# Tail tokens of the first token mixing as half-row pairs, u products in another pool, the last store on ScalarE's queue

## The chip, the cores and the metric

One Trainium2 chip, one of its cores. The kernel is one launch. Its time is the device time in microseconds of one execution, as the median of several runs. A profile of one further execution comes with it.

## The reference

For 8 batches, 8 heads, 576 tokens and a head size of 64: a linear attention with cosine weights, then an MLP mixer over tokens and channels. All in float32, matmuls of the kernel in bfloat16.

```python
def _attn_ref(q, k, v):                       # q, k, v: (8, 8, 576, 64)
    theta = pi/2 * pos / S
    phi(x) = concat([relu(x) * cos(theta), relu(x) * sin(theta)], -1)   # 128 features
    kv  = einsum('bhsf,bhsd->bhfd', phi(k), v);   z = sum(phi(k), axis=2)
    num = einsum('bhsf,bhfd->bhsd', phi(q), kv)
    den = einsum('bhsf,bhf->bhs', phi(q), z)[..., None] + 1e-06
    return num / den

def _moe_ref(x, w_tok1, w_tok2, w_ch1, w_ch2):    # x: (8, 576, 512), the heads side by side
    xt = x.transpose(0, 2, 1)
    h  = relu(xt @ w_tok1) @ w_tok2               # 576 -> 256 -> 576 tokens
    u  = x + h.transpose(0, 2, 1)
    h2 = relu(u @ w_ch1) @ w_ch2                  # 512 -> 1536 -> 512 channels
    return u + h2
```

## The kernel before

**Tokens.** The 576 tokens of a batch are four chunks of 128 (ci = 0 to 3) and a tail of 64 (ci = 4, called R). A chunk's tile has tokens on the 128 partitions and 512 channels (8 heads of 64) on the free axis. The tail's 64 tokens are stored twice as broad: partitions 0 to 63 hold the tail's tokens with heads 0 to 3, partitions 64 to 127 the same tokens with heads 4 to 7, so its tile is 128 x 256. `half(g)` names the partitions of half g.

**Front and channel.** Each batch has a *front* (class `Front`: attention and token mixing) and a *channel* part (class `Channel`: channel mixing and the store). While TensorE does the channel part of batch b, the pieces of the front of batch b+1 are put between its steps. The channel part is a list of 38 steps: 12 c steps (slots C+0 to C+11; `c_main` L418: 4 matmuls of 512 columns for 128 of the 1536 hidden channels, `c_tail` L428 the same for the tail tokens, 64 columns) and then the o steps (slots O+0 and on, O = 12): chunk 0 in 6 parts of 2 matmuls (L444), the tail in two halves (L448: 12 matmuls of 256 columns, each on 64 of the array's columns), then chunks 1, 2, 3 in 6 parts each. The last batch does its tail last. `pieces()` gives each piece of the next front a slot, after which it is issued; batch 1's front (made during batch 0's channel part) has a plan of its own, `first=True`. The order on each engine is the order of issue written out here.

**The front's stages.** `feature` (L193, VectorE) makes phi(k) and phi(q); `values` casts v and stands beside a column of ones; `kv` (L213) multiplies them, for the tail with the two halves of the array's rows, two accumulators in turn; `kv_out` copies to SBUF; `q_trans` or a transposing DMA brings phi(q) to feature-major form. `num` (L252, tail L259 with 64 columns each) gives numerator and denominator of a chunk in `num_ps`; VectorE makes x from it with three operations (L265 add, L266 reciprocal, L267 multiply). `tok1` (L280, tail L284) is the first token mixing: `b1_ps[mi]`, mi = 0 and 1, each 128 of the 256 hidden tokens x 512 channels, summed over the five chunks. The tail part uses `w_tail1`, which holds the last 64 rows of w_tok1 in the partitions of half g and zeros in the others: a matmul over all 128 rows then picks half g. That is two matmuls of 256 columns per mi. `tok1_out` is the relu, on ScalarE (L290) for mi = 0 and on VectorE (L292) for mi = 1. `tok2` (L308, tail L312) is the second token mixing into `u_ps`; VectorE adds x (L315), ScalarE casts to bfloat16 (L316), and u is transposed by DMA (in the first two fronts on TensorE, `u_trans`, L322).

**Pools of PSUM.** `ps_mm` has 4 buffers: c_ps, ct_ps, o_ps, b1_ps, transposes, and u_ps for batches from 1 on. `ps_at` has 2: kv_ps, num_ps, large transposes, and u_ps in the first front. 

**The first front** (batch 0, `first_front`) has no channel part beside it. It keeps TensorE occupied with matmuls on zeros (L163) while the first loads come, and runs num of one chunk, then tok1 of the chunk before it.

**Slots of the token mixing before**, batches 2 to 7: num of chunks 0, 1, 2 after C+9, C+10, C+11, of the tail after O+1, of chunk 3 after O+3; tok1 of all but chunk 3 after O+4 (mi = 0) and O+5 (mi = 1); tok1 of chunk 3 and the relus after O+6; tok2 from O+8 to O+12.

**Stores.** Each output chunk is added on VectorE (L454) and stored by a DMA issued by SP (L456); the tail's two halves are two DMAs, both issued by SP (L460).

Of the kernel before, what the change touches and what calls it, by code (L numbers as in the profile page):

```python
# [10 lines left out]
BF16 = mybir.dt.bfloat16  # L11
# [5 lines left out]
def kernel(  # L17
# [15 lines left out]
    nc = tc.nc  # L33

    B, H, S, D = q.shape
    F = 2 * D
    Dm = H * D
    S_tok, D_tok = moe_w_tok1.shape
    Dm2, D_ch = moe_w_ch1.shape
    P = 128  # L40
    R = S // P
    SM = R * P
    ST = S - SM
    NSC = R + 1
    NCC = Dm // P
    NT = D_tok // P
# [3 lines left out]
    DH = Dm // 2  # L50
    assert S_tok == S and Dm2 == Dm and F == P and 2 * ST == P and H == 2 * HH


    ORDER = (0, 1, 2, R, 3)

    def half(g):
        return slice(g * ST, (g + 1) * ST)


    const = ctx.enter_context(tc.tile_pool(name="const", bufs=1))  # L60
# [3 lines left out]
    once = ctx.enter_context(tc.tile_pool(name="once", bufs=1))  # L64
# [59 lines left out]

    w_tok1 = const.tile([P, R, D_tok], BF16, name="w_tok1")

    w_tail1 = const.tile([P, 2, D_tok], BF16, name="w_tail1")
    for g in range(2):
        nc.vector.memset(w_tail1[half(1 - g), g, :], 0.0)
    w_tok2n = const.tile([P, NT, S], BF16, name="w_tok2n")  # L130
    w_tok2 = const.tile([P, NT, S], BF16, name="w_tok2")
    w_ch1 = const.tile([P, NCC, D_ch], BF16, name="w_ch1")
    w_ch2 = const.tile([P, NCH, Dm], BF16, name="w_ch2")
    for g in range(2):
        nc.gpsimd.dma_start(out=w_tail1[half(g), g, :], in_=moe_w_tok1[SM:S, :])
    after(nc.gpsimd.dma_start(out=w_tok1,
                              in_=moe_w_tok1[0:SM, :].rearrange("(p r) t -> p r t", r=R)),
          k_done)
# [32 lines left out]
    class Front:  # L171
# [96 lines left out]
                self.x[:, ci, 0:n * DH].rearrange("p (g j d) -> p g j d", g=n, j=HH),  # L268
                nv[:, :, :, 0:D], den.to_broadcast([P, n, HH, D]))

        def tok1(self, mi, chunks):
            if not hasattr(self, "B1"):
                self.B1 = once.tile([P, NT, Dm], BF16, name="B1")
                self.b1_ps = {}
            if mi not in self.b1_ps:
                self.b1_ps[mi] = ps_mm.tile([P, Dm], F32, name="b1_ps", tag="mm")
            cols = slice(mi * P, (mi + 1) * P)
            for ci in chunks:
                if ci < R:
                    nc.tensor.matmul(self.b1_ps[mi], w_tok1[:, ci, cols], self.x[:, ci, :],  # L280
                                     start=(ci == 0), stop=(ci == R - 1))
                else:
                    for g in range(2):
                        nc.tensor.matmul(self.b1_ps[mi][:, g * DH:(g + 1) * DH],  # L284
                                         w_tail1[:, g, cols], self.x[:, R, 0:DH],
                                         start=False, stop=False, skip_group_check=True)

        def tok1_out(self, mi, on_act=True):
            if on_act:
# [60 lines left out]
            self.values(ci, nc.vector)  # L350
            self.q_side(ci)

        def mix_head(self, mi):
            self.tok1(mi, ORDER[:-1])

        def mix_tail(self):
            for mi in range(NT):
                self.tok1(mi, ORDER[-1:])
                self.tok1_out(mi, on_act=(mi == 0))

        def pieces(self, first=False):


            F, V, KV, N = self.features, self.values, self.kv, self.num
            KS, QS, QT, T, U = self.k_side, self.q_side, self.q_trans, self.tok2, self.u_trans
            C, O = 0, NCH
            if first:

                plan = [(C + 2, KS, 0), (C + 2, KS, 1), (C + 3, KS, 2), (C + 3, KS, 3),
                        (C + 4, KS, 4), (C + 4, V, 0, nc.vector), (C + 4, V, 1, nc.vector)]  # L370
                plan += [(C + 5, V, ci, nc.vector) for ci in (2, 3, 4)]
                plan += [(C + 6 + ci, KV, ci) for ci in range(NSC)]
                plan += [(C + 7 + ci, QS, ci, ci % 2 == 1) for ci in range(NSC)]
                plan.append((C + 10, self.kv_out))
                plan += [(C + at, QT, ci) for ci, at in enumerate((9, 10, 11, 12, 13))]
            else:
                plan = [(C + ci, V, ci, nc.scalar) for ci in range(NSC)]
                plan += [(C + at, KS, ci) for ci, at in enumerate((0, 0, 1, 2, 2))]
                for ci, at in enumerate((1, 2, 3, 4, 5)):
                    plan += [(C + at, QS, ci), (C + at, self.q_trans_dma, ci)]  # L380
                plan += [(C + at, KV, ci) for ci, at in enumerate((2, 3, 4, 6, 7))]
                plan.append((C + 8, self.kv_out))
            if first:
                plan += [(O + at, N, ci) for ci, at in zip(ORDER, (2, 4, 7, 9, 11))]
                mix, t = O + 13, O + 17
            else:
                plan += [(at, N, ci) for ci, at in zip(ORDER, (C + 9, C + 10, C + 11, O + 1, O + 3))]
                mix, t = O + 4, O + 8
            plan += [(mix, self.mix_head, 0), (mix + 1, self.mix_head, 1),
                     (mix + 2, self.mix_tail)]  # L390
            if first:
                plan += [(t, T, 0), (t + 1, T, 1), (t + 2, T, 2), (t + 3, U, 0), (t + 3, T, 3),
                         (t + 4, U, 1), (t + 4, T, 4), (t + 5, U, 2), (t + 6, U, 3),
                         (t + 7, U, 4)]
            else:
                plan += [(t + ci, T, ci) for ci in range(NSC)]
                plan += [(t + 1, self.u_trans_dma, 0, 2), (t + 4, self.u_trans_dma, 2, NSC)]
            slots = {}
            for slot, what, *args in sorted(plan, key=lambda p: p[0]):
                slots.setdefault(slot, []).append((what, args))  # L400
            return slots
# [4 lines left out]
    class Channel:  # L406
# [28 lines left out]
        def o_step(self, ci, part, parts):  # L435
            b, res = self.b, self.res
            if part == 0:
                self.o_ps = ps_mm.tile([P, Dm], F32, name="o_ps", tag="mm")
            o_ps = self.o_ps
            each = NCH // parts  # L440
            for ki in range(each * part, each * (part + 1)):
                start, stop = ki == 0, ki == NCH - 1
                if ci < R:
                    nc.tensor.matmul(o_ps, self.h1T[:, ki, ci * P:(ci + 1) * P], w_ch2[:, ki, :],  # L444
                                     start=start, stop=stop)
                    continue
                for g in range(2):
                    nc.tensor.matmul(o_ps[half(g), 0:DH], self.h1T[:, ki, SM:S],  # L448
                                     w_ch2[:, ki, g * DH:(g + 1) * DH], start=start, stop=stop)
            if part < parts - 1:  # L450
                return
            n = Dm if ci < R else DH
            o_sb = small.tile([P, Dm], F32, name="o_sb")
            nc.vector.tensor_add(o_sb[:, 0:n], o_ps[:, 0:n], res["u"][:, ci, 0:n])  # L454
            if ci < R:
                nc.sync.dma_start(  # L456
                    out=out[b, 0:SM, :].rearrange("(p r) d -> p r d", r=R)[:, ci, :], in_=o_sb)
                return
            for g in range(2):
                nc.sync.dma_start(out=out[b, SM:S, g * DH:(g + 1) * DH], in_=o_sb[half(g), 0:DH])  # L460

        def steps(self, done):

# [19 lines left out]
    def first_front(f):  # L483

        idle_ps = ps_at.tile([P, 512], F32, name="idle_ps", tag="at")
        busy(idle_ps, 16)
        for ci, heads in [*((c, (0, HH)) for c in range(R)), *((c, (HH, H)) for c in range(R)),
                          (R, None)]:
            f.feature("q", ci, 0, heads)
            f.feature("q", ci, 1, heads)  # L490
            f.q_trans(ci, heads)
            busy(idle_ps, 1)
        busy(idle_ps, 18)
        for ci in range(NSC):
            f.k_side(ci)
        for ci in range(NSC):
            f.values(ci, nc.vector if ci in (1, 3) else nc.scalar)
        for ci in range(NSC):
            f.kv(ci)
        f.kv_out(split=True)  # L500
        busy(idle_ps, 2)
        for ki in range(NT):
            permute_tok2(ki)
        for i in range(NSC + 1):
            if i < NSC:
                f.num(ORDER[i], fill=1)
            if i > 0:
                for mi in range(NT):
                    f.tok1(mi, ORDER[i - 1:i])
        for mi in range(NT):  # L510
            f.tok1_out(mi, on_act=(mi == 0))

        c = Channel(0, f.res)
        for ci in range(NSC + 2):
            if 2 < ci - 1 <= R:
                for mi in range(AHEAD):
                    c.c_main(mi, (ci - 4) * P, (ci - 3) * P)
            if ci < NSC:
                f.tok2(ci, ps_at)
            if ci > 1:  # L520
                f.u_trans(ci - 2, nc.scalar if ci == 3 else nc.vector)
        for ci in range(2, R):
            for mi in range(AHEAD):
                c.c_main(mi, ci * P, (ci + 1) * P)
        return c
# [60 lines left out]
```

## Time and profile before

| | |
|---|---|
| median of 3 runs | 282.4 us (282.09 to 282.59) |
| the profiled execution | 281.66 us, its span 279.9 us |
| granted TensorE clock | 0.999 |
| busy TensorE (PE), VectorE, ScalarE | 266.1, 161.1, 123.1 us |
| L444 and L418, the two large groups of matmuls | 94.7 and 95.1 us |
| L284, the tail of the first token mixing | 32 matmuls, 5.9 us busy, mean 272 ns |
| L308 and L312, u products | 19.0 and 3.3 us |

The span is the time from the first to the last instruction of the profiled execution. Busy time of TensorE counts the full length of each matmul, from its start to the arrival of its last result, so neighbours overlap: a 512-column matmul has a length of 380 ns, while the next starts 216 ns after it. What a matmul costs on a busy TensorE is therefore read from starts to starts, not from lengths. PEld is the loading of weights, which runs beside the matmuls.

### The profile page before, as it was taken

What the parts mean: (1) busy time and instruction counts of PE and PEld (TensorE: products, weight loads), DVE (VectorE), ACT (ScalarE), POOL (GpSimd) and SP (SyncE); (2) the same over time, 40 slices, a digit from 0 to 9 for tenths busy, and PEclk for the clock granted to TensorE, in tenths of its full rate; (3) what the DMA queues carried; (4) which work ended last, traced back from release to release, by engine and by line L of the source; (5) the groups of instructions that cost most, each with busy time, mean ns of one, the idle gap of its engine ahead of it and who ended that gap; (6) DMA issues with size and microseconds to landing.
All of it is one profiled execution on the core that took longest, in us unless ns stands there. A gap on an engine that the chain in (4) does not pass through costs nothing.

```text
span 279.9 us, 5799 instructions
## 1 busy us (share of the span) xinstructions
PE 266.1 (95%) x2345; PEld 143.8 (51%) x2370; DVE 161.1 (58%) x395; ACT 123.1 (44%) x237; POOL 9.7 (3%) x20
## 2 busy tenths in 40 slices
PE   5987899999999999999999999999999999999993
PEld 2653666545554455545554455545554455545542
DVE  2877781857576494557566485558467576540021
ACT  2642569048723186036624185137614274225500
POOL 3240020000000000000000000000000000000000
PEclk9999999999999999999999999999999999999999
DMA  6999999921779945992789648994789653161012
GB/s 170 347 192 256 340 181 267 358 89 40 163 215 341 178 112 128 341 294 101 161 257 328 177 103 121 354 267 128 134 260 319 183 96 75 59 160 40 0 75 94
DMA packets 90010, 52.51 MB, mean 188 GB/s; under 512 B 57216, under 2 KB 85760, under 8 KB 89984
## 3 DMA queue, kind: packets, MB, share of 16 engines
q1 hardware_dynamic: 86736, 48.38, 63.1%
q0 software_dynamic: 3248, 3.77, 8.2%
q8 instruction: 18, 0.29, 0.4%
q14 instruction: 8, 0.07, 0.1%
HBM read 35.85 MB, written 9.44 MB: 162 GB/s over the span
## 4 chain that ended last, share of the span: by engine, by line
PE 91%; DVE 3%; ACT 2%; issue 1%; POOL 0%; POOLq 0%; ACTq 0%
PE o_ps L444 29%; PE c_ps L418 29%; PE u_ps L308 5%; PE o_ps L448 5%; PE b_ps L280 4%; PE idle_ps L163 4%; PE ct_ps L428 4%; PE kv_ps L213 4%; PE num_ps L252 3%; PE b_ps L284 1%; ACT qpT L237 1%; DVE x_sb L267 1%; PE qT_ps L235 1%; DVE u_sb L315 1%; PE u_ps L312 1%
## 5 line engine op out<-in xcount | busy, mean ns | idle before, releaser
L444 PE MATMUL o_ps<-w_ch,h1T 128*128 128x512 bf16 x368 | 94.7, 380 | 0.8
L418 PE MATMUL c_ps<-uT,w_ch 128*128 128x512 bf16 (+1 forms) x420 | 95.1, 361 | 0.0
L422 ACT ACTIVATE h1T<-c_ps 128x512 bf16<-128x512 f32 x96 | 57.4, 602 | 62.3 <-PE c_ps L418 62.2
L454 DVE TENSOR_TENSOR o_sb<-o_ps,u_sb 128x512 f32<-128x512 f32 (+1 forms) x40 | 25.5, 637 | 49.4 <-PE o_ps L444 47.7
L444 PEld LDWEIGHTS <-h1T 128*128 128x128 bf16 x384 | 34.5, 98 | 36.3 <-issue 2.6
L418 PEld LDWEIGHTS <-w_ch 128*128 128x128 bf16 x420 | 34.3, 98 | 27.4
L316 ACT CAST u_bf<-u_sb 128x512 bf16<-128x512 f32 (+1 forms) x40 | 22.3, 575 | 21.0 <-DVE u_sb L315 14.5
L428 PEld LDWEIGHTS <-w_ch 128*128 128x128 bf16 x384 | 22.0, 98 | 18.6
L315 DVE TENSOR_TENSOR u_sb<-u_ps,x_sb 128x512 f32<-128x512 f32 (+1 forms) x40 | 25.4, 637 | 9.4 <-PE u_ps L308 7.5
L267 DVE TENSOR_TENSOR x_sb<-num_ps,den 128x512 bf16<-128x512 f32 (+1 forms) x40 | 25.5, 638 | 1.4
L290 ACT ACTIVATE B<-b_ps 128x512 bf16<-128x512 f32 x8 | 4.8, 597 | 47.2 <-PE b_ps L280 47.2
L265 DVE TENSOR_SCALAR den<-num_ps 128x8 f32<-128x8 f32 (+1 forms) x40 | 6.6, 165 | 32.6 <-PE num_ps L252 32.0
L428 PE MATMUL ct_ps<-uT,w_ch 128*128 128x64 bf16 x384 | 24.1, 193 | 0.0
L193 DVE TENSOR_SCALAR qp<-qt,cos_t 128x512 bf16<-128x512 f32 (+1 forms) x44 | 18.8, 431 | 3.0 <-DMA qt<-in_q_dram 3.0
L308 PE MATMUL u_ps<-B,w_tok 128*128 128x512 bf16 x64 | 19.0, 379 | 1.0 <-ACT B L290 0.7
L201 ACT CAST v_aug<-vt 128x512 bf16<-128x512 f32 (+1 forms) x33 | 18.8, 577 | 1.9 <-DMA vt<-in_v_dram 1.9
L193 DVE TENSOR_SCALAR kp<-kt,cos_t 128x512 bf16<-128x512 f32 (+1 forms) x40 | 18.3, 459 | 0.8 <-DMA kt<-in_k_dram 0.8
L280 PE MATMUL b_ps<-x_sb,w_tok 128*128 128x512 bf16 x57 | 16.4, 380 | 1.9 <-DVE x_sb L267 1.8
L193 DVE TENSOR_SCALAR kp<-kt,sin_t 128x512 bf16<-128x512 f32 (+1 forms) x40 | 18.1, 452 | 0.0
L193 DVE TENSOR_SCALAR qp<-qt,sin_t 128x512 bf16<-128x512 f32 (+1 forms) x42 | 18.0, 429 | 0.0
L163 PE MATMUL idle_ps<-zeros,ident 128*128 128x512 bf16 x43 | 12.4, 420 | 3.4 <-DVE zeros L159 3.2
L213 PE MATMUL kv_ps<-v_aug,kp 128*128 128x65 bf16 (+1 forms) x320 | 15.4, 194 | 0.0
(54 smaller groups left out, 173.2 us busy)
## 6 DMA issues: line engine op xcount, KB each, us to landing
kt<-in_k_dram SPq DMA_DIRECT2D x8, 1024.0 KB, 6.7
vt<-in_v_dram SPq DMA_DIRECT2D x8, 1024.0 KB, 7.9
out_dram<-o_sb SPq DMA_DIRECT2D x32, 256.0 KB, 2.5
qt<-in_q_dram SPq DMA_DIRECT2D x7, 1024.0 KB, 7.6
w_ch<-in_moe_w_ch_dram POOLq DMA_DIRECT2D x4, 384.0 KB, 9.4
w_ch<-in_moe_w_ch_dram POOLq DMA_DIRECT2D x3, 512.0 KB, 8.0
qt<-in_q_dram SPq DMA_DIRECT2D x16, 64.0 KB, 6.7
qt<-in_q_dram SPq DMA_DIRECT2D x2, 512.0 KB, 5.0
```

Source lines behind the costliest of these rows:

```text
L163: nc.tensor.matmul(dst, ident, zeros[:, 0:dst.shape[-1]], start=True, stop=True)
L193: nc.vector.tensor_scalar(o_ap, i_ap, scalar1=w, scalar2=0.0, op0=ALU.mult, op1=ALU.max)
L213: nc.tensor.matmul(self.kv_ps[:, g, j * D1:(j + 1) * D1], self.kp[ci][rows, i, :, :].rearrange("p a b -> p (a b)"), self.va[rows, ci, i, : ...
L267: nc.vector.tensor_mul(self.x[:, ci, 0:n * DH].rearrange("p (g j d) -> p g j d", g=n, j=HH), nv[:, :, :, 0:D], den.to_broadcast([P, n, HH, ...
L280: nc.tensor.matmul(self.b1_ps[mi], w_tok1[:, ci, cols], self.x[:, ci, :], start=(ci == 0), stop=(ci == R - 1))
L308: nc.tensor.matmul(u_ps, w_tok2[:, ki, ci * P:(ci + 1) * P], self.B1[:, ki, :], start=(ki == 0), stop=(ki == NT - 1))
L315: nc.vector.tensor_add(res["u"][:, ci, 0:n], u_ps[:, 0:n], self.x[:, ci, 0:n])
L418: nc.tensor.matmul(c_ps[:, lo:hi], w_ch1[:, ki, mi * P:(mi + 1) * P], uT[:, lo // P:hi // P, ki, :], start=(ki == 0), stop=(ki == NCC - 1))
L422: nc.scalar.activation(self.h1T[:, mi, 0:SM], c_ps, AF.Relu)
L428: nc.tensor.matmul(self.ct_ps[:, mi % 6, :], w_ch1[:, ki, mi * P:(mi + 1) * P], self.res["uT"][:, R * NCC + ki % 2, half(ki // 2)], start= ...
L444: nc.tensor.matmul(o_ps, self.h1T[:, ki, ci * P:(ci + 1) * P], w_ch2[:, ki, :], start=start, stop=stop)
L454: nc.vector.tensor_add(o_sb[:, 0:n], o_ps[:, 0:n], res["u"][:, ci, 0:n])
```

## The change

1. `w_tail1` becomes one tile with the last 64 rows of w_tok1 in both halves of the partitions and no zeros; the two memsets go. `tok1_tail(k)` issues a pair of matmuls, each over 64 rows: for mi = 0 with half k of the rows into half k of the columns of `b1_ps[0]`, for mi = 1 with the other half into the other half of the columns of `b1_ps[1]`. k = 0 and k = 1 make up what the four matmuls of L284 did.
2. The order of chunks in the token mixing becomes 0, 1, R, 2, 3, with new slots. Batches 2 to 7: num of chunks 0, 1, R after C+9, C+10, C+11, of 2 after O+1, of 3 after O+4; `mix_head` (tok1 of chunks 0 and 1, first pair) after O+3, `mix_body` (chunk 2) after O+5, `mix_tail` (chunk 3 for mi = 0, second pair, relu, chunk 3 for mi = 1, relu) after O+6; tok2 from O+8 as before. Batch 1: num after O+2, O+4, O+7, O+8, O+11 where it was O+2, O+4, O+7, O+9, O+11 for the order 0, 1, 2, R, 3; mixing after O+9, O+12, O+13 where it was O+13, O+14, O+15; tok2 from O+16 where it was O+17. The first front issues its pairs likewise.
3. The u products of batches 2 to 7 take their PSUM buffer from `ps_at`.
4. The very last store (half 1 of the last batch's tail) is issued by ScalarE.

```diff
-    ORDER = (0, 1, 2, R, 3)
+    ORDER = (0, 1, R, 2, 3)
...
-    w_tail1 = const.tile([P, 2, D_tok], BF16, name="w_tail1")
-    for g in range(2):
-        nc.vector.memset(w_tail1[half(1 - g), g, :], 0.0)
+    w_tail1 = const.tile([P, D_tok], BF16, name="w_tail1")
...
-        nc.gpsimd.dma_start(out=w_tail1[half(g), g, :], in_=moe_w_tok1[SM:S, :])
+        nc.gpsimd.dma_start(out=w_tail1[half(g), :], in_=moe_w_tok1[SM:S, :])
...
+        def tok1(self, mi, ci):
...
+            nc.tensor.matmul(self.b1_ps[mi], w_tok1[:, ci, mi * P:(mi + 1) * P], self.x[:, ci, :],
+                             start=(ci == 0), stop=(ci == R - 1))
+
+        def tok1_tail(self, k):
+            for mi in range(NT):
+                g = (mi + k) % 2
+                nc.tensor.matmul(self.b1_ps[mi][:, g * DH:(g + 1) * DH],
+                                 w_tail1[half(g), mi * P:(mi + 1) * P], self.x[half(g), R, 0:DH],
+                                 start=False, stop=False, skip_group_check=True)
...
-        def mix_head(self, mi):
-            self.tok1(mi, ORDER[:-1])
+        def mix_head(self):
+            for mi in range(NT):
+                for ci in ORDER[:2]:
+                    self.tok1(mi, ci)
+            self.tok1_tail(0)
+
+        def mix_body(self):
+            for mi in range(NT):
+                self.tok1(mi, ORDER[-2])
 
         def mix_tail(self):
             for mi in range(NT):
-                self.tok1(mi, ORDER[-1:])
+                self.tok1(mi, ORDER[-1])
+                if mi == 0:
+                    self.tok1_tail(1)
                 self.tok1_out(mi, on_act=(mi == 0))
...
-                plan += [(O + at, N, ci) for ci, at in zip(ORDER, (2, 4, 7, 9, 11))]
-                mix, t = O + 13, O + 17
+                at, mix, t = (O + 2, O + 4, O + 7, O + 8, O + 11), O + 9, O + 16
             else:
-                plan += [(at, N, ci) for ci, at in zip(ORDER, (C + 9, C + 10, C + 11, O + 1, O + 3))]
-                mix, t = O + 4, O + 8
-            plan += [(mix, self.mix_head, 0), (mix + 1, self.mix_head, 1),
-                     (mix + 2, self.mix_tail)]
+                at, mix, t = (C + 9, C + 10, C + 11, O + 1, O + 4), O + 3, O + 8
+            plan += [(i, N, ci) for i, ci in zip(at, ORDER)]
+
+            plan += [(mix, self.mix_head), (at[-1] + 1, self.mix_body), (at[-1] + 2, self.mix_tail)]
...
-                plan += [(t + ci, T, ci) for ci in range(NSC)]
+                plan += [(t + ci, T, ci, ps_at) for ci in range(NSC)]
...
-                nc.sync.dma_start(out=out[b, SM:S, g * DH:(g + 1) * DH], in_=o_sb[half(g), 0:DH])
+                eng = nc.scalar if b == B - 1 and g == 1 else nc.sync
+                eng.dma_start(out=out[b, SM:S, g * DH:(g + 1) * DH], in_=o_sb[half(g), 0:DH])
...
+                if ORDER[i - 1] == R:
+                    f.tok1_tail(0)
+                    continue
                 for mi in range(NT):
-                    f.tok1(mi, ORDER[i - 1:i])
+                    f.tok1(mi, ORDER[i - 1])
+                    if (mi, i) == (0, NSC):
+                        f.tok1_tail(1)
```

More of the change, by code (lines that the diff above doesn't have):

```diff
@@ L51 @@
     assert S_tok == S and Dm2 == Dm and F == P and 2 * ST == P and H == 2 * HH
-    ORDER = (0, 1, 2, R, 3)
+    ORDER = (0, 1, R, 2, 3)
+    assert NT == 2 and R == 4
     def half(g):
@@ L269, in num @@
                 nv[:, :, :, 0:D], den.to_broadcast([P, n, HH, D]))
[L271 to L275, printed above, removed]
-                self.b1_ps[mi] = ps_mm.tile([P, Dm], F32, name="b1_ps", tag="mm")
[L277 to L286, printed above, removed]
+        def tok1(self, mi, ci):
+            if ci == 0:
+                if mi == 0:
+                    self.B1 = once.tile([P, NT, Dm], BF16, name="B1")
+                    self.b1_ps = {}
+                self.b1_ps[mi] = ps_mm.tile([P, Dm], F32, name="b1_ps", tag="mm")
+            nc.tensor.matmul(self.b1_ps[mi], w_tok1[:, ci, mi * P:(mi + 1) * P], self.x[:, ci, :],
[6 more added lines that the diff above has]
+                                 start=False, stop=False, skip_group_check=True)
         def tok1_out(self, mi, on_act=True):
@@ L351, in features @@
             self.q_side(ci)
-        def mix_head(self, mi):
-            self.tok1(mi, ORDER[:-1])
+        def mix_head(self):
[6 more added lines that the diff above has]
+                self.tok1(mi, ORDER[-2])
         def mix_tail(self):
             for mi in range(NT):
-                self.tok1(mi, ORDER[-1:])
+                self.tok1(mi, ORDER[-1])
+                if mi == 0:
+                    self.tok1_tail(1)
                 self.tok1_out(mi, on_act=(mi == 0))
```

## The prediction

> **What bounds the kernel now.** I read the page first: busy shares, then the chain that ended last.
>
> ```profile
> PE 266.1 (95%) x2345; PEld 143.8 (51%) x2370; DVE 161.1 (58%) x395; ACT 123.1 (44%) x237; POOL 9.7 (3%) x20
> ...
> PE 91%; DVE 3%; ACT 2%; issue 1%; POOL 0%; POOLq 0%; ACTq 0%
> ```
>
> TensorE (PE) is busy 95% of the span and carries 91% of the chain. From batch 1 on the pattern repeats every 31.13 us (the first half of L448 starts at 146.48, 177.60 and 208.73 in the timeline), and in that pattern PE waits for almost nothing. The list of waits has one entry for the u products, 0.3 us in the whole run:
>
> ```profile
> PE u_ps L308 <- DVE u_sb L315: 0.3, 1, 0.3
> ```
>
> So in six of the eight batches the question is only how long PE itself takes for the edited matmuls. What PE loses between its instructions is seen in its timeline, where it goes from full matmuls to halves of the array. First rows in halves (kv, 64*128), beside a full kv chunk (128*128):
>
> ```profile
> 165.81 0.28 PE L428 MATMUL ct_ps<-uT,w_ch 128*128 128x64 bf16 x4
> 165.92 0.42 PE L213 MATMUL kv_ps<-v_aug,kp 128*128 128x65 bf16 x8
> 166.18 1.02 PE L418 MATMUL c_ps<-uT,w_ch 128*128 128x512 bf16 x4
> 167.04 0.28 PE L428 MATMUL ct_ps<-uT,w_ch 128*128 128x64 bf16 x4
> 167.26 0.30 PE L213 MATMUL kv_ps<-v_aug,kp 64*128 64x65 bf16 x8
> 167.49 1.04 PE L418 MATMUL c_ps<-uT,w_ch 128*128 128x512 bf16 x4
> ```
>
> The columns are start and length in us. From ct to the next c it takes 0.37 with eight full kv matmuls, 0.45 with eight half ones. The half ones start 0.22 after ct instead of 0.11, so 0.11 is lost on the way in. Then the columns in halves (128*64), with the present tail products (L284):
>
> ```profile
> 175.99 0.38 PE L284 MATMUL b_ps<-x_sb,w_tail 128*128 128x256 bf16 x2
> 176.21 0.59 PE L444 MATMUL o_ps<-w_ch,h1T 128*128 128x512 bf16 x2
> ...
> 177.29 0.38 PE L284 MATMUL b_ps<-x_sb,w_tail 128*128 128x256 bf16 x2
> 177.60 0.85 PE L448 MATMUL o_ps<-w_ch,h1T 128*64 128x256 bf16 x12
> 178.38 0.39 PE L280 MATMUL b_ps<-x_sb,w_tok 128*128 128x512 bf16 x1
> ...
> 183.16 0.59 PE L444 MATMUL o_ps<-w_ch,h1T 128*128 128x512 bf16 x2
> 183.68 0.41 PE L312 MATMUL u_ps<-B,w_tok 128*64 128x256 bf16 x4
> 184.03 5.79 PE L444 MATMUL o_ps<-w_ch,h1T 128*128 128x512 bf16 x25
> ```
>
> Two full tail products cost 0.22 (175.99 to 176.21), 0.11 each; a 512-column matmul 0.216. On the way into halves: 177.29 + 0.22 = 177.51, but L448 starts at 177.60; 183.16 + 0.43 = 183.59, but L312 starts at 183.68: 0.09 each. Inside: six pairs take 0.78 (177.60 to 178.38), two take 0.35, so a pair of 256-column halves adds 0.43/4 = 0.11, as one full matmul does, and 0.13 is left over for the return.
>
> **The change, part by part.**
>
> *Tail products as pairs.* Per batch four full matmuls (4 x 0.11 = 0.43) become two pairs, and each pair stands alone between full matmuls: the first behind the chunk 0 and 1 products of step O+3, the second between the two last-chunk products. Each pays the way in, the pair and the way back: 0.09 + 0.11 + 0.13 = 0.33 by the column rows. By the kv rows: 0.45 less the 0.11 that ct to c takes with nothing between (164.83 to 164.94 in the same timeline) is 0.34, less four pairs at about 0.03 leaves 0.20 to 0.22 for both switches, plus 0.11 is 0.31 to 0.33. Against the 0.22 that two full ones cost, a pair loses 0.09 to 0.12; I take 0.10, nearest the kv rows, which split the rows as the new pairs do. Six batches x 2 pairs x 0.10 = **+1.2** (0.95 to 1.45). Nothing covers it: PE is the path.
>
> The Trainium skill ("TensorE: Matmul & The Clock Gate", "Measured speedup vs the span model") gives a pack of tiles one matmul's time plus about 4 ns for each further tile, with no charge for coming and going; by that a pair would take 0.11, and 14 pairs would save 1.5 us. Its "TensorEngine Tiling (Array Packing)", "Key Properties", speaks against this change: a change of tiling mode drains the engine; the gaps of 0.09 to 0.13 above bear out the second and show the first inside a long run of pairs only.
>
> *Order 0, 1, R, 2, 3 and the moved steps, batches 2 to 7.* The num product of the tail chunk stands behind the last ct matmuls instead of behind an o step: one excursion in either place, 0. The num of chunk 3 moves from O+3 to O+4, its use stays at O+6. From its last matmul to its use PE has 0.43 (o) + 0.43 (chunk 2) + 0.87 (half of L448 with its switches) = 1.73. VectorE needs 0.23 to start, 1.13 for the three operations and 0.05 to report, 1.41: hidden with 0.3 to spare. The second pair delays both relus and the u products alike. 0.
>
> *u products in the pool of num, batches 2 to 7.* With two buffers u(i+2) waits for the add of u(i): that add starts 180.77 and takes 0.69, done 181.46, and u(2) starts at 181.86 in the timeline. Hidden with 0.4 to spare; it frees a place in the other pool for which nothing waits. 0.
>
> *Batch 1's mixing (under batch 0's channel steps).* Two pairs +0.2. The tail num product now follows the second half of L448 directly, both in halves of the columns, so one way in and back falls away: -0.2. Chunk 3's num stays at O+11 while its use comes at O+13 instead of O+15: 3 x 0.43 = 1.30 of PE work against 1.41, a wait of 0.1. Steps T and U come one step earlier: 0 to 0.2, as a transposed copy on ScalarE then releases a buffer. Sum **+0.1** (-0.1 to +0.4).
>
> *First front (batch 0).* Here VectorE is the path:
>
> ```profile
> 23.01 0.17 DVE L265 TENSOR_SCALAR den<-num_ps 128x8 f32<-128x8 f32 x1 [0.31 <-PE num_ps L252]
> ...
> 23.45 0.69 DVE L267 TENSOR_TENSOR x_sb<-num_ps,den 128x512 bf16<-128x512 f32 x1
> ...
> 24.20 0.38 PE L280 MATMUL b_ps<-x_sb,w_tok 128*128 128x512 bf16 x1 [0.78 <-DVE x_sb L267]
> ...
> 24.82 0.69 DVE L292 TENSOR_SCALAR B<-b_ps 128x512 bf16<-128x512 f32 x1 [0.68 <-PE b_ps L280]
> 25.26 1.12 PE L308 MATMUL u_ps<-B,w_tok 128*128 128x512 bf16 x4 [0.69 <-ACT B L290]
> ```
>
> The four tail products now run while PE waits for x, free. Afterwards one pair stands between the two last-chunk products, on the path to the relu of L292: +0.31. With the tail third in order VectorE's gap of 0.31 ahead of the last chunk shrinks to about 0.2 and moves: -0.1. Sum **+0.2** (-0.1 to +0.35). The two memsets (0.33 us) go from ahead of a 3.0 us wait of VectorE for the first load: 0.
>
> *Last store.* Two stores are issued one behind the other on SP; the program's end waits for them.
>
> ```profile
> 276.11 1.13 SPq L460 DMA_DIRECT2D out_dram<-o_sb  x2
> ```
>
> The waits of SP show what the second costs:
>
> ```profile
> SPq L581 <- DMA out_dram<-o_sb: 1.2, 2, 0.6
> ```
>
> Two waits at the end, 0.6 each: the second store lands 0.6 after the first. Issued from ScalarE, idle since 264.5, both go at 276.11. No row shows a DMA issued by ScalarE: nothing gained if it is slow to start, 0.85 if the closing waits also overlap it; nearest are SP's own pair: **-0.55**. That part works as meant.
>
> Sum: 1.2 + 0.1 + 0.2 - 0.55 = **+0.95 us**. The profiled execution took 281.66 (span 279.9 and 1.8 around it), 0.74 below the median 282.4 of the runs; it would come to 282.6, the median to **283.35**.
>
> **The rivals.**
>
> *Switching is free, the pairs run as a gain (faster).* If the array passes between full and half-row matmuls without loss, a pair costs 0.11 and saves 0.11: in the 14 pairs of batches 1 to 7 -1.5, with the store's -0.55 and -0.2 in batch 1's order about 280.2. It decides where both ways together cost under 0.11. Against it: the 0.11 ahead of every half-row kv group and 0.09 ahead of L448 and L312. For it: tails of 256 columns in half rows are not in the trace. 0.10. (It is the case of the span model cited above from "TensorE: Matmul & The Clock Gate" in the Trainium skill.)
>
> *The pairs don't overlap (the change doesn't do what it says).* The second of a pair then adds 0.11: 14 x 0.11 = +1.5 on top, 284.9. Against it: eight half-row kv matmuls fit in 0.23 with the way back. For it: there, 65 columns each, not 256. 0.08.
>
> *The losses cancel.* The store gains 0.85, the fronts nothing, and a pair loses 0.08: 12 x 0.08 - 0.85 = +0.1, 282.5. 0.10.
>
> **How the numbers follow.** A measurement of this kernel tells about 0.2% (0.56 us) from no change. The forecast has 0.72; its own bounds run from 0.95 - 0.1 - 0.1 - 0.85 = -0.1 to 1.45 + 0.4 + 0.35 = +2.2, most of it between +0.2 and +1.7. Of it 0.10 lies within 0.56. Slower: 0.62 + 0.08 = 0.70; same: 0.10 + 0.10 = 0.20; faster: 0.10. The range 282.3 to 284.3 holds the forecast and the cancelling case and leaves out the free switch and the serial pairs.
>
> **What would show it.** Right: the period of L448 grows from 31.13 to about 31.33; in the timeline each pair of L285 of the new kernel is followed by a full matmul 0.2 after its start and preceded by a gap of 0.1; the two starts of a pair lie together; SP's two last waits become one of 0.6. Wrong: a period at or below 31.13, or PE waiting for x of chunk 3 or for u adds in batches 2 to 7, where I count none.

## The result, and the profile after

The changed kernel takes 284.25 us (median of 4 runs, 283.86 to 284.79) against 282.25 us of the kernel before (4 runs): ratio 1.0064, 95% interval 1.0044 to 1.0083, so slower by 1.2 to 2.3 us. The forecast was +0.95, below that interval; the time itself lies in the range by 0.05 us. The profiled execution took 284.25 us, its span is 282.5 (before 281.66 and 279.9). On the page of the changed kernel TensorE is still busy 95%. In the chain that ended last a DMA share of 13% has appeared: the chain now runs through loads, one of them told below.

```profile
PE 268.1 (95%) x2345; PEld 143.2 (51%) x2370; DVE 160.0 (57%) x393; ACT 123.2 (44%) x237; POOL 11.5 (4%) x20
...
PE 79%; DMA 13%; SPq 2%; POOL 2%; issue 1%; DVE 0%; ACT 0%; POOLq 0%
```

The timeline of TensorE in the changed kernel, around the token mixing of one batch (columns: start, length, engine, line, operation, xcount):

```profile
177.90 0.28 PE L285 MATMUL b_ps<-x_sb,w_tail 64*128 64x256 bf16 x2
178.11 0.61 PE L453 MATMUL o_ps<-w_ch,h1T 128*128 128x512 bf16 x2
...
179.24 0.59 PE L276 MATMUL b_ps<-x_sb,w_tok 128*128 128x512 bf16 x2
179.77 0.85 PE L457 MATMUL o_ps<-w_ch,h1T 128*64 128x256 bf16 x12
180.55 0.39 PE L276 MATMUL b_ps<-x_sb,w_tok 128*128 128x512 bf16 x1
180.87 0.28 PE L285 MATMUL b_ps<-x_sb,w_tail 64*128 64x256 bf16 x2
181.40 0.85 PE L457 MATMUL o_ps<-w_ch,h1T 128*64 128x256 bf16 x12 [0.25 <-issue]
182.18 0.60 PE L453 MATMUL o_ps<-w_ch,h1T 128*128 128x512 bf16 x2
```

The pair of L285 starts 0.32 after the product of L276 ahead of it (180.55 to 180.87), where a full matmul follows in 0.216: 0.10 lost on the way in. From the pair to the next full matmul it is 0.21 (177.90 to 178.11), of which 0.11 is the pair: 0.10 on the way back. The two starts of a pair lie 3 ns apart in the trace. From the first half of L457 to the second, the two last-chunk products and the pair between them take 0.85 (180.55 to 181.40): 3 x 0.11 for the three changes of form, the rest for the work. The trace has no matmul record of the second last-chunk product; its weight load stands at 181.08, so it ran between the pair and L457, where the timeline marks 0.25 as issue.

A *change of form* means here that TensorE goes from matmuls on the full array to matmuls on half of its rows or half of its columns, back again, or from one kind of half to the other. The weight loads in the same trace show the loss too. Without such a change the load for the next matmul starts 2 ns after the start of the matmul ahead (179.243 and 179.245 us). For the first pair above it starts 307 ns after the start of the full product ahead (177.588 and 177.895), which is 0.09 after the 0.216 of that product, and the pair's first matmul starts 4 ns behind it.

The repeat is now 31.34 long (179.77, and 211.10 for the next batch), where it was 31.13.

The stretch in the first front, where the pair stands between the two last-chunk products:

```profile
24.65 0.38 PE L276 MATMUL b_ps<-x_sb,w_tok 128*128 128x512 bf16 x1 [0.66 <-DVE x_sb L266]
...
24.96 0.28 PE L285 MATMUL b_ps<-x_sb,w_tail 64*128 64x256 bf16 x2
...
25.17 0.39 PE L276 MATMUL b_ps<-x_sb,w_tok 128*128 128x512 bf16 x1
...
25.60 0.69 DVE L293 TENSOR_SCALAR B<-b_ps 128x512 bf16<-128x512 f32 x1 [1.00 <-PE b_ps L276]
```

The second product comes 0.52 after the first instead of 0.21, and the relu on VectorE waits 1.00 instead of 0.68. The last stores, in the timeline of the end and in SP's list of waits (line, what it waited for: us in all, times, longest):

```profile
279.01 0.49 SPq L470 DMA_DIRECT2D out_dram<-o_sb  x1
279.02 0.54 ACTq L470 DMA_DIRECT2D out_dram<-o_sb  x1
```

```profile
SPq L596 <- DMA out_dram<-o_sb: 1.6, 2, 0.9
```

Both go at the same time; SP still waits twice. SP's own store lands 1.95 after its issue, ScalarE's 2.21.

**The sum over the two traces.** All but the start can be read by counting from the first add of VectorE on a num product (L265, L264 in the changed kernel), since from there on each kernel repeats closely, but for one load (below).

| stretch | before | after | difference |
|---|---|---|---|
| first instruction to first add of num | 18.67 | 19.23 | +0.56 |
| to the first c product (first front) | 9.76 | 9.98 | +0.22 |
| to the first o tail | 21.08 | 21.85 | +0.77 |
| first to last o tail (mixing of batches 1 to 7) | 224.61 | 225.96 | +1.35 |
| last o tail to the end (stores) | 5.77 | 5.46 | -0.30 |

The second, fourth and fifth lines are what the prediction was about: +1.27. The first and third, +1.33 together, it did not have. The third is one wait of TensorE, for the weights of the second channel product in batch 0, in the changed kernel's timeline:

```profile
48.65 0.59 PE L453 MATMUL o_ps<-w_ch,h1T 128*128 128x512 bf16 x2
49.85 0.59 PE L453 MATMUL o_ps<-w_ch,h1T 128*128 128x512 bf16 x2 [0.61 <-DMA w_ch<-in_moe_w_ch_dram]
```

So two things were to be settled: whether the 0.21 per batch are the changes of form, and whether the other 1.33 belong to the edit.

### The profile page after: what moved, and what is told of

Read it like the earlier page. It is cut to its first block, busy times and chain, and to the rows that moved or that the text cites. A ratio compares the mean times of both kernels' runs of the same rounds, so it can differ in the third digit from the quotient of the medians.

```text
span 282.5 us, 5797 instructions
## 1 busy us (share of the span) xinstructions
PE 268.1 (95%) x2345; PEld 143.2 (51%) x2370; DVE 160.0 (57%) x393; ACT 123.2 (44%) x237; POOL 11.5 (4%) x20
## 4 chain that ended last, share of the span: by engine, by line
PE 79%; DMA 13%; SPq 2%; POOL 2%; issue 1%; DVE 0%; ACT 0%; POOLq 0%
PE o_ps L453 29%; PE c_ps L427 26%; DMA w_ch<-in_moe_w_ch_dram 7%; PE o_ps L457 4%; PE b_ps L276 4%; PE u_ps L309 4%; PE ct_ps L437 3%; DMA vt<-in_v_dram 3%; PE num_ps L251 3%; DMA kt<-in_k_dram 3%; PE kv_ps L212 3%; SPq L82 1%; PE b_ps L285 1%; POOL w_ch L148 1%; PE u_ps L313 1%
## 5 line engine op out<-in xcount | busy, mean ns | idle before, releaser
L453 PE MATMUL o_ps<-w_ch,h1T 128*128 128x512 bf16 x369 | 95.2, 380 | 1.5 <-DMA w_ch<-in_moe_w_ch_dram 0.6
L453 PEld LDWEIGHTS <-h1T 128*128 128x128 bf16 x384 | 33.9, 98 | 37.9 <-issue 3.5
L264 DVE TENSOR_SCALAR den<-num_ps 128x8 f32<-128x8 f32 (+1 forms) x40 | 6.6, 164 | 42.9 <-PE num_ps L251 40.2
L276 PE MATMUL b_ps<-x_sb,w_tok 128*128 128x512 bf16 x57 | 16.8, 380 | 2.1 <-DVE x_sb L266 2.1
L162 PE MATMUL idle_ps<-zeros,ident 128*128 128x512 bf16 x43 | 13.4, 449 | 2.9 <-DVE zeros L158 2.7
```

Of the source, the lines that this page charges most:

```text
L276: nc.tensor.matmul(self.b1_ps[mi], w_tok1[:, ci, mi * P:(mi + 1) * P], self.x[:, ci, :], start=(ci == 0), stop=(ci == R - 1))
```

## Experiments

Ratios are to the kernel before, run beside each kernel on the same chip: its median was 282.51 us (35 runs) beside the first four kernels, 282.8 (12 runs) beside the changed kernel run again and the last three kernels. The period is that of the o tail, from the start of its first matmul in one batch to that in the next. The *first transposes* are TensorE's first matmuls on loaded data, of the first front's q. S, M and Q are the theories named in the first expectation.

**The store alone.** The kernel before with

```diff
-                nc.sync.dma_start(out=out[b, SM:S, g * DH:(g + 1) * DH], in_=o_sb[half(g), 0:DH])
+                eng = nc.scalar if b == B - 1 and g == 1 else nc.sync
+                eng.dma_start(out=out[b, SM:S, g * DH:(g + 1) * DH], in_=o_sb[half(g), 0:DH])
```

> The kernel before with only the last store issued by ScalarE. Three theories of the changed kernel's +2.0 us. S (switches and chance): the pairs cost +0.2 us per batch, and the later clock rise and the later first loads in the changed kernel's profile are chance of the single runs. M (memsets): the removed memsets let the warm-up start earlier and so the clock and the loads come later, every time. Q (queue): that ScalarE issues a DMA at all sets up something at the start that delays the loads. S and M expect here 281.9 us (before 282.25, less 0.36 as the last landing comes 0.36 earlier), period of the o tail 31.13. Q expects 282.5 to 283.2, with the first transposes at 8.7 us or later and the c products of the first channel part waiting 0.8 us for their weights.

282.03 us, ratio 0.998 (0.9965 to 0.9995). Period 31.127, first transposes at 8.35, no wait for weights; from the last o tail to the end 5.46 instead of 5.77. Neither the late start nor the wait that theory Q expects is in this profile, and the time is not the one it expects; the store is worth 0.30.

**Full tail products in the new order.** The changed kernel with

```diff
-                nc.tensor.matmul(self.b1_ps[mi][:, g * DH:(g + 1) * DH],
-                                 w_tail1[half(g), mi * P:(mi + 1) * P], self.x[half(g), R, 0:DH],
+                nc.tensor.matmul(self.b1_ps[mi][:, g * DH:(g + 1) * DH],
+                                 w_tail1[:, g, mi * P:(mi + 1) * P], self.x[:, R, 0:DH],
```

and `w_tail1` with its zeros again.

> The changed kernel with each pair made of two full matmuls over 128 rows again (zeros in the other half, memsets back); order, slots, pool and store as changed. If the pairs' switches are the 0.2 us per batch, the period of the o tail falls from 31.34 to 31.12 to 31.14, and the whole to 281.9 to 282.4 (282.25 with -0.36 for the store, +0.1 to +0.3 for the order in the first two fronts). If instead the new order or the pool were what slowed the batches, the period stays at 31.3 and the time at 283.5 or more. Q expects the late start here too (+0.6 to +1.3), S and M do not.

281.85 us, ratio 0.9984 (0.9963 to 1.0004). Period 31.13 in four of five batches, 31.16 in the other. Its timeline at the place of the second pair:

```profile
148.28 0.39 PE L278 MATMUL b_ps<-x_sb,w_tok 128*128 128x512 bf16 x1
148.50 0.38 PE L287 MATMUL b_ps<-x_sb,w_tail 128*128 128x256 bf16 x2
149.03 0.85 PE L459 MATMUL o_ps<-w_ch,h1T 128*64 128x256 bf16 x12
```

The full tail products follow the chunk's product in 0.22, and the way to the second half of L459 is 0.75 (148.28 to 149.03) instead of 0.85; here too the second last-chunk product has no record. In four of the five periods the order, the slots and the pool cost nothing, and the pairs alone make the 0.21 per batch. First to last o tail takes 224.55 here, 0.06 less than before, and the first front 9.885, 0.12 more. The first transposes come at 9.36, the latest of all fourteen profiles, with the memsets in place: the removed memsets of theory M are not what makes a start late. A late start is what theory Q expects here; but a profile of the kernel before, with no store on ScalarE, has one of 9.17 (below).

**The pair beside a half.** The changed kernel with

```diff
             for mi in range(NT):
                 self.tok1(mi, ORDER[-1])
-                if mi == 0:
-                    self.tok1_tail(1)
+            self.tok1_tail(1)
+            for mi in range(NT):
                 self.tok1_out(mi, on_act=(mi == 0))
```

> The changed kernel with the second pair moved behind the last chunk's second product, so that it stands directly ahead of the second column half of the o tail. If only the change between full and half arrays costs (about 0.1 us each way), two of eight changes go: period 31.34 - 0.20 = 31.14. If a change from half rows to half columns costs as much as any other, one goes: period 31.23 to 31.25, and the time falls by 7 x 0.1 = 0.7 us against the changed kernel, to about 283.0 to 283.5. If the loss of a pair is not its switches but its own length, the period stays 31.34.

283.01 us, ratio 1.0014 (0.9992 to 1.0036). Period 31.23.

```profile
147.36 0.61 PE L276 MATMUL b_ps<-x_sb,w_tok 128*128 128x512 bf16 x2
147.90 0.28 PE L285 MATMUL b_ps<-x_sb,w_tail 64*128 64x256 bf16 x2
148.11 0.85 PE L457 MATMUL o_ps<-w_ch,h1T 128*64 128x256 bf16 x12
148.89 0.39 PE L453 MATMUL o_ps<-w_ch,h1T 128*128 128x512 bf16 x1
```

From the pair to the column half it is 0.21 (147.90 to 148.11), as from a pair to a full matmul: going from half rows to half columns is one change like any other. One of the changes is gone, and the period is 0.106 shorter. Not the length of a pair but the number of changes counts. (The eight changes of the expectation are those of the pairs and the o tail alone.)

**The memsets back.** The changed kernel with

```diff
     w_tail1 = const.tile([P, D_tok], BF16, name="w_tail1")
+    spare = const.tile([P, 2, D_tok], BF16, name="spare")
+    for g in range(2):
+        nc.vector.memset(spare[half(1 - g), g, :], 0.0)
```

> The changed kernel with the two memsets back, on a tile that nothing reads. M expects the first transposes at 8.14 instead of 8.70 us in the profile, and 0.5 to 1.3 us less than the changed kernel: 282.9 to 283.7. S expects nothing from it: 283.5 to 284.4 by the chance of the start, period 31.34.

284.08 us, ratio 1.0055 (1.0034 to 1.0076), where the changed kernel run again (next) has 1.0057. The first transposes come at 8.41, in the kernel with the pair beside the half, which has no memsets, at 7.47. M falls.

One of the five periods is 31.47 instead of 31.34, and the list of waits has this entry:

```profile
PEld L261 <- DMA qpT<-qp: 0.2, 1, 0.2
```

This is the num product of the tail (L258 in the changed kernel), which the new order moved from O+1 to C+11. Its weights come from a transposing DMA that landed at 173.74 us; their load started 0.13 later than in the other batches. In the same batch of the changed kernel's four profiles this DMA landed 0.06 to 0.6 ahead of the load, in the three of the kernel before 1.4 to 1.7 ahead. The new order has taken most of that slack.

**The changed kernel again**, the same code:

> The changed kernel once more. S (what the change itself costs is what the lines of the two profiles account for: first front +0.22, mixing of seven batches +1.36, end -0.30, sum +1.28; the rest of +2.0, a late clock rise and a wait of 0.77 for the weights of the second channel product, is chance of single runs): ratio 1.0045, 283.6 to 284.0 where the kernel before is 282.5, no wait for those weights in this profile, first transposes anywhere between 7.5 and 9.4 us as in the other profiles. If the rest belongs to the change: 284.3 or more, the wait for the weights there again.

284.59 us (6 runs), ratio 1.0057 (1.0035 to 1.0079). The first transposes came at 7.69, earlier than before's 8.14, but TensorE then waited 1.52 for the first k features, and the first add of num was later still, at 19.99; and the wait for the weights was there again, 0.75 long. Both the median and the wait's return are what was expected if the rest belongs to the edit (284.3 or more). But the kernel before was slower beside it too, at 282.8, and the ratio's interval holds the 1.0045 of S. Four more profiles were taken to tell the two apart.

> The changed kernel, one more profile for its first 52 us. Up to the place of the wait of 0.75 for the weights of the second channel product, this kernel, the one with the second pair beside the half, and the changed kernel's two earlier profiles run the same instructions; two of these three had the wait. If it is chance of the loads: it goes with the landing of the first k load (12.8 us and later in the two that waited, 11.9 in the one that did not), and need not be here. If it belongs to the changed kernel: it is here again.

> As the run before it, a second time. Both together: by chance, at least one without the wait is likely; as a property of the kernel, both with it. The period stays 31.34 in either case.

> The kernel before, one more profile for its first 52 us: by chance of the loads, a first k load that lands at 12.8 us or later brings the same wait for the weights here (the need comes 0.2 earlier than in the changed kernel); as a property of the changed kernel, no wait here at any landing.

> As the run before it, a second time. The period is 31.13, and the first transposes lie anywhere between 7.5 and 9.4 us in both.

Both further profiles of the changed kernel (284.11 and 282.86 us; the kernel before 282.69 and 282.11) are without the wait. The same place in the second of them:

```profile
48.00 1.02 PE L453 MATMUL o_ps<-w_ch,h1T 128*128 128x512 bf16 x4
```

where four matmuls of L453 run in one piece. So it is chance in the sense that the same instructions meet it or not: two of the changed kernel's four profiles have it. The kernel with the pair beside the half runs the same instructions up to there; counted in, it is two of five. The first k load does not tell which: the issue by GpSimd that waits for it started at 12.81 and 13.65 with the wait, at 13.49 and 11.90 without, so that part of the expectation fell. What goes with the wait is the issue by GpSimd (POOL) of the three loads of these weights, here in the changed kernel's first profile (with the wait) and its third (without):

```profile
36.07 4.29 POOL L148 DMA_DIRECT2D w_ch<-in_moe_w_ch_dram  x3 [18.20 <-DMA vt<-in_v_dram]
...
36.02 2.51 POOL L148 DMA_DIRECT2D w_ch<-in_moe_w_ch_dram  x3 [17.47 <-DMA vt<-in_v_dram]
```

It took 4.3 and 4.8 us in the two with the wait, and the last load was issued at 39.6 and 40.4; in the other twelve profiles of this study 2.4 to 2.7 us, and not after 37.8. Why the issue is slow at times stays open, and so does whether it is rarer in the kernel before, which has none in three profiles.

With these profiles the stretch from the first add of num to the end can be compared without the start:

| | first transposes | first add of num | from there to the end |
|---|---|---|---|
| before | 8.14, 9.17, 8.46 | 18.67, 19.69, 19.10 | 261.21, 261.23, 261.23 |
| changed, no wait for the weights | 8.86, 8.05 | 19.83, 18.57 | 262.51, 262.50 |
| changed, with the wait | 8.70, 7.69 | 19.23, 19.99 | 263.26, 263.23 |

From the first add on, the profiles of each row repeat to 0.03, and the edit costs +1.28. The first add scatters by 1.0 us in the three profiles of the kernel before and by 1.4 in the four of the changed one. The edit doesn't move it on average: in the seven profiles that run the instructions of the kernel before up to there the mean is 19.19, in the five with the changed kernel's (the one with the pair beside the half among them) 19.19 too.

**The column halves in one piece.** The kernel before with the store on ScalarE and

```diff
             plan += [(mix, self.mix_head, 0), (mix + 1, self.mix_head, 1),
-                     (mix + 2, self.mix_tail)]
+                     (mix + 2 if first else mix + 1, self.mix_tail)]
```

> The kernel before with the last store on ScalarE and the second part of the mixing one step earlier (ahead of the o tail, not between its halves), so that the 24 matmuls in halves of the columns run in one piece: two of ten changes per batch fall away in six batches, nothing else. S, 0.1 us a change: period 31.13 - 0.20 = 30.93, time 282.5 - 1.2 - 0.3 = 281.0. If a pair loses for another reason than the changes, or the second entry is free because the weights of the halves are still known: period 31.13, 282.2. If chunk 3's x is now late: period above 30.93 with PE waiting for VectorE's multiply.

281.35 us, ratio 0.9948 (0.9927 to 0.9969). Period 30.90.

```profile
146.85 0.59 PE L280 MATMUL b_ps<-x_sb,w_tok 128*128 128x512 bf16 x2
147.37 1.50 PE L448 MATMUL o_ps<-w_ch,h1T 128*64 128x256 bf16 x24
148.81 0.39 PE L444 MATMUL o_ps<-w_ch,h1T 128*128 128x512 bf16 x1
```

24 matmuls take 1.44 (147.37 to 148.81); in two pieces of 12 they took 0.78 each, and each piece had its way in besides. Two changes fewer, 0.227 less, and TensorE's list of waits has none for x of chunk 3 in these batches.

**All column halves together.** The kernel before with the store on ScalarE and

```diff
-            for ci in ((0, R, 1, 2, 3) if self.b < B - 1 else range(NSC)):
+            for ci in ((0, R, 1, 2, 3) if self.b == 0 else (R, 0, 1, 2, 3) if self.b < B - 1 else range(NSC)):
...
-                plan += [(O + at, N, ci) for ci, at in zip(ORDER, (2, 4, 7, 9, 11))]
+                plan += [(O + at, N, ci) for ci, at in zip((0, 1, R, 2, 3), (2, 4, 7, 9, 11))]
```

> The kernel before with the last store on ScalarE and, in batches 1 to 6 of the channel part, the o tail ahead of chunk 0, so that its 24 matmuls and the num products of the next front's tail (both on halves of the columns) run in one piece; in batch 0 the next front's tail num goes directly behind the o tail. Four of ten changes per batch fall away in six batches, two in batch 1's mixing. S: period 31.13 - 0.40 = 30.73, time 282.5 - 2.4 - 0.2 - 0.3 = 279.6. If the o tail waits for the relu of the last ct products: about 0.3 of it comes back per batch, 281.4, with PE waiting for ScalarE ahead of L448.

279.32 us, ratio 0.9882 (0.9862 to 0.9902): faster than the kernel before by 1.0 to 1.4%, and than the changed kernel run beside it (284.59). Period 30.67 in four of five batches, 30.83 in the other.

```profile
140.57 0.42 PE L252 MATMUL num_ps<-kv_sb,qpT 128*128 128x65 bf16 x8
140.92 1.50 PE L448 MATMUL o_ps<-w_ch,h1T 128*64 128x256 bf16 x24
142.25 0.29 PE L259 MATMUL num_ps<-kv_sb,qpT 128*64 128x65 bf16 x8
142.71 0.81 PE L444 MATMUL o_ps<-w_ch,h1T 128*128 128x512 bf16 x3 [0.16 <-issue]
```

The num products of the tail (L259) follow the o tail with no gap, since both use halves of the columns, and the o tail follows num of chunk 2 in 0.35: nothing waits for the relu. Four changes fewer, 0.454 less per batch.

**One store for the last tail.** The kernel before with

```diff
+            if b == B - 1:
+                nc.sync.dma_start(out=out[b, SM:S, :].rearrange("t (g d) -> g t d", g=2),
+                                  in_=o_sb[:, 0:DH])
+                return
```

> The kernel before with the two stores of the last tail as one DMA of 128 rows by SP. If what the second store costs is its issue and its place behind the first (0.6 in SP's last waits), the end comes 0.5 to 0.6 earlier: 5.2 us from the start of the last o tail to the end instead of 5.77. If a store's landing grows with its rows, 5.4 to 5.5, as with the store on ScalarE (5.46).

One run, 284.65 us: 8.13 from the last o tail to the end instead of 5.77, outside both expectations. SP's closing waits, and the DMA row of the window from 275 to 283 us (40 slices, digits in tenths of 16 engines):

```profile
SPq L585 <- DMA out_dram<-o_sb: 4.1, 2, 3.6
```

```profile
DMA  0000000999400001011011111111111000000000
```

The store is issued at 276.74. Its data run from 278.0 to 281.2, 3.2 us, at a tenth of the DMA engines' time. The Trainium skill ("DMA: Bandwidth & Descriptors", "Why a DMA increments its semaphore by 16 and not by 1") says that a DMA is spread over at most 16 engines by its slowest dimension, a number that divides both sides; here that is the 2 of the halves on the side of the output, and two of 16 engines are 0.125, which agrees with the row of ones. So this run tells of the form of the access (the halves as the outer dimension), not of one store in place of two, and that question stays open.

## Why the prediction was right, and where it was not

The mechanism was right: TensorE is the path, and a lone pair loses two changes of form. That the time itself fell in the range was partly luck, as the last paragraph of this section tells.

Per batch, in six batches, the prediction had 2 x 0.10 = 0.20; the period shows 0.21. The price came from the right rows: both ways of the half-row kv group at 0.20 to 0.22, and each change measures 0.107 now. That can be checked over five kernels. Count the changes per batch (kv tail 2, o tail 4, tail num 2, tail u 2: ten before). Where two pairs replace four tail products, the matmuls themselves take 0.217 less, if a pair counts as one full matmul of 256 columns:

| | changes | period | per change against before |
|---|---|---|---|
| changed | 14 | 31.337 | (0.210 + 0.217) / 4 = 0.107 |
| pair beside a half | 13 | 31.231 | (0.104 + 0.217) / 3 = 0.107 |
| before; new order with full tails | 10 | 31.127; 31.13 | |
| halves in one piece | 8 | 30.900 | 0.227 / 2 = 0.114 |
| halves together | 6 | 30.673 | 0.454 / 4 = 0.114 |

Removing a change is worth about as much as adding one costs. The rival by which switching is free is refuted in both directions, and so is the one by which pairs don't overlap (their starts are 3 ns apart). The two pages of the Trainium skill stand as weighed: the 4 ns for a further tile of "TensorE: Matmul & The Clock Gate" ("Measured speedup vs the span model") holds inside a pair, with 3 ns here, and the drain of "TensorEngine Tiling (Array Packing)" ("Key Properties") agrees with the loss of 0.11 at each change, also between half rows and half columns.

*Order, slots and pool in batches 2 to 7, predicted 0*: 31.13 with full tails in the new order; TensorE's list of waits has no x of these batches and no add. What the sum overlooked is the transposing DMA ahead of the moved num of the tail: it costs nothing in the changed kernel's four profiles, and 0.13 in one batch of the run with the memsets back. *Batch 1's mixing, +0.1*: 225.96 - 224.61 is +1.35, less 6 x 0.21 leaves +0.09. Its parts came otherwise: the wait of 0.1 for x of chunk 3 is not in the list, and in its place stands one for a transposed copy on ScalarE, which the prediction had put at 0 to 0.2:

```profile
PE u_ps L313 <- ACT uT L328: 0.2, 1, 0.2
```

*First front, +0.2*: +0.22, and 0.12 with full tails in the pair's place, which are 0.10 shorter.

*Last store, -0.55*: -0.30, the term that was mis-sized. It took the second store's 0.6 in SP's waits for the whole gain and assumed that ScalarE's store lands as SP's does. ScalarE's store lands 2.21 after its issue, where SP's second store of the kernel before took 2.04 and was issued 0.54 later: it lands 0.37 earlier, and the program ends 0.30 earlier. SP's closing waits did not become one of 0.6, as foretold, but stayed two, 1.6 in all. The range (0 to -0.85) held it, and the rival in which the losses cancel, which needed 0.85 here and free fronts, falls with it. The sum thus is +1.28 and not +0.95.

The time of 284.25 was still at the upper end of the range (284.3), because the prediction used one profiled execution for the start and said nothing of what varies in it. The first add of num came anywhere between 18.35 and 19.99 us in the fourteen profiles of all kernels here, and the wait for the second channel weights adds 0.75 in some. In the first comparison the profile of before (281.66) was 0.6 below the median of its runs, and the profiled execution of the changed kernel had the wait. The runs give +1.2 to +2.3 and +1.0 to +2.2 in the two comparisons, and +0.96 to +2.15 for the changed kernel with its memsets back; +1.28 lies in all three, in their lower part, as it has to if the wait comes in some of the runs. That the rest of the measured difference is this wait and the start is argued from the profiles; the unprofiled runs don't show it. The forecast of 283.35 was thus too low by the store and by what it left out of the start, and the range held the result by little: that part was luck.

## What to carry to other kernels

On a busy TensorE count the changes between the full array, halves of the rows and halves of the columns, at 0.11 us each in this kernel, before splitting a matmul into a pair: a lone pair of 256 columns saves 0.11 and pays two changes. Whether a pair pays beside others on half rows no run here shows. For the halves that a kernel has anyhow the order of steps counts: putting those of the columns together took 2.8 us off this kernel (3.07 from the first add of num to the end, less 0.30 for the store). And compare two kernels from a point behind the start: 1.4 us of scatter there hides an effect of 1.3.

## What was not expected of the hardware

The start of the clock. TensorE's first matmuls of 512 columns start 427 ns apart, and at some point 216 ns: at 5.2 to 8.7 us after the first instruction in the fourteen profiles, at 7.80 and 5.67 for the same kernel, so within a stretch of 3.5 us. The first of these matmuls starts at 2.73 without the memsets and at 3.21 with them. The mean granted clock of the profiled runs (0.996 to 1.0) does not show it. The Trainium skill ("TensorE: Matmul & The Clock Gate", "What's actually happening") gives a window of 3.4 us that runs free of the kernel's start; the spread agrees with it.

A store issued by ScalarE took 0.54 us to issue and 2.21 to land, one by SP at the same moment 0.49 and 1.95.

A store of 128 rows whose output side begins with a dimension of 2 moved its data in 3.2 us at the share of about two of the DMA engines, where two stores of 64 rows each landed within 2.0 of their issue.
